# A GQA decode kernel's prologue reordered: q product between the two layer norms, constants ahead of x, residual copies behind the MLP's first half

## Chip, cores, metric

One core of one Trainium2 chip runs the whole program. The metric is the device time of one execution in microseconds (us); a median of several runs is given.

In the views PE is TensorE's matrix engine, PEld its weight loads, DVE VectorE, ACT ScalarE and SPq the queue of the SyncE. Evacuating is copying a result out of PE's output memory. The granted clock is the share of PE's full clock in the profile's records; half clock is a record of 0.5. L294 is the helper that waits for a semaphore.

## The reference

One decode step for four sequences: a layer norm `xn` of `x`; attention of `xn @ wq` with 16 query heads over 8 cached K/V heads of 8192 rows by 256; an MLP block on `xn`; the two are multiplied and added to `x`.

```python
xn = _layernorm(x)                       # x: (4, 1, 448)
s = _A_ref(xn, k_cache, v_cache, wq, wo) # K and V caches: (4, 8, 8192, 256) each, bf16
#   q = xn @ wq;  p = softmax(q k^T / 16);  o = p v;  s = o @ wo
g = _silu(_B_ref(xn, w1, w2, w3, w4))
#   x1 = xn + (shifted gelu(...)) ;  g = x1 + gelu(layernorm(x1) @ w3) @ w4
#   with one position the shifts leave only zeros, so x1 = xn and w1, w2 are not needed
return x + s * g
```

The K and V caches are 32 tiles each of 4.19 MB: 268 of the 279 MB that the program reads.

## The kernel before

A short prologue makes q and the MLP; then PE transposes each K tile, multiplies it with q and multiplies the probabilities with V. One queue (the SyncE's) issues all loads but that of x, in one fixed order:

```python
# SyncE: wq, w3, w4, then
load_k(0); load_k(1)                  # K0 (in two halves) and K1: no wait
load_wo(NLATE, HQ, "dwo")             # most of wo: no wait
for h in range(2, NH):
    load_k(h)                         # waits v_k >= h - 1: tile h-2 has been evacuated
    load_v(h - 2)                     # waits v_v: the V buffer is free
```

The prologue on VectorE (DVE), in the old order, and PE's part beside it:

```python
c(v.memset(q_ps[:, 0:QW], 0.0))
v.wait_ge(S["dx"], 16)
c(v.tensor_copy(x_f[:, :], x_sb[:, :]))
layernorm(x_f, xn_f, xn_b, 0, 1)          # each: sums, a square root on ACT, six copies
layernorm(xn_f, xn2_f, xn2_b, 8, 2)
c(v.tensor_reduce(par[:, :], idv, AX.X, ALU.add))
for k, dst in ((0, xnT), (1, xn2T)):      # four multiplications for each turn
    v.wait_ge(S["p_x"], k + 1)
    ...
# four memsets; sel, selb (reductions of the identity)
v.wait_ge(S["p_q"], 1)
v.tensor_copy(q_b[:, :], q_ps[:, 0:QW])   # then the residual copies x4, xn4
v.wait_ge(S["p_h"], 1)                    # MLP: gelu_u, tanh on ACT, hT, second product ...
...
# PE: turn xn, turn xn2, q product (28 matmuls), MLP's first product (49), q's transposes,
#     MLP's second product (14), a sum (4), four warm-up products (result unused), then K0's transposes
```

Of the kernel before, what the change touches and what calls it, by code (L numbers as in the profile page):

```python
# [7 lines left out]
ALU = mybir.AluOpType  # L8
AX = mybir.AxisListType
# [54 lines left out]
def bass_recurrent_scan__gqa_block_cached__mixer_s_mlp__decode_kernel(  # L64
# [13 lines left out]
    Bn, Sq, D = A_x.shape  # L78
    _, HKV, SK, DH = A_k_cache.shape
    HD = A_wq.shape[1]  # L80
    HQ = HD // DH
    REP = HQ // HKV
    F = B_w3.shape[1]
    assert Sq == 1 and REP == 2 and DH == 2 * P and HD == HQ * DH
    NHF = 2
# [6 lines left out]
    NQD = 4  # L92
    NDG = 2
    DQ, PQ = D // NDG, P // NQD
    DP = NDG * PQ
    assert D == NDG * DQ
    NCH = SK // P
# [12 lines left out]
    NCG = 4  # L110
    CGW = P // NCG
    CP = 2
# [23 lines left out]
    with ExitStack() as es:  # L136
        def sb(name, shape, dty):
# [7 lines left out]
        ident_f = sb("ident_f", [P, P], F32)  # L145
# [6 lines left out]
        selb = sb("selb", [P, PQ], F32)  # L152
        q_b = sb("q_b", [P, QW], BF16)
        pT = sb("pT", [P, 2, NCH * REP + PVW], BF16)
        xnT = sb("xnT", [P, DK, NHF, Bn], BF16)
        xn2T = sb("xn2T", [P, DK, NHF, Bn], BF16)
        par = sb("par", [P, NHF], F32)
        hT = sb("hT", [P, NFK, NHF, Bn], BF16)
        sel = sb("sel", [P, CP, PVW], F32)
# [11 lines left out]
        x_f = sb("x_f", [Bn, D], F32)  # L171
        xn_f = sb("xn_f", [Bn, D], F32)
        xn_b = sb("xn_b", [Bn, DK, P // 2, 2], BF16)
        xn2_f = sb("xn2_f", [Bn, D], F32)
        x4 = sb("x4", [DP, DQ], F32)
        xn4 = sb("xn4", [DP, DQ], F32)
        sg4 = sb("sg4", [DP, DQ], F32)
        res = sb("res", [DP, DQ], F32)
        xn2_b = sb("xn2_b", [Bn, DK, P // 2, 2], BF16)
# [6 lines left out]
        psc = [es.enter_context(nc.psum_tensor("psc%d" % i, [P, 512], F32)) for i in range(2)]  # L186
        psm = es.enter_context(nc.psum_tensor("psm", [P, 512], F32))
        psv = es.enter_context(nc.psum_tensor("psv", [P, 512], F32))
# [13 lines left out]
                                                                k=NFK)  # L202
# [15 lines left out]
                                                 r=REP)  # L218
# [74 lines left out]
        def take(eng, name, n=1):  # L293
            return eng.wait_ge(S[name], n).then_inc(S[name], -n)  # L294

        NPI, NPC = 4, 13

        def prog_pool(gp):
            c = _Chain(gp, S["g_c"])
            c(gp.memset(ident_f[:, :], 0.0))  # L300
            c(gp.memset(ident_b[:, :], 0.0))
            c.sync()
            for t in (ident_b, ident_f):
                c(gp.affine_select(out=t[:, :], in_=t[:, :], compare_op=ALU.not_equal, fill=1.0,
                                   base=0, pattern=[[-1, P]], channel_multiplier=1))
            c(gp.memset(ones_f[:, :], 1.0))
            c(gp.memset(diag[:, :], 0.0))
            c(gp.memset(sel[:, :, :].rearrange("p c n -> p (c n)"), 0.0))
            c(gp.memset(rz[:, :, :].rearrange("p s r -> p (s r)"), 1.0))
            gp.wait_ge(S["v_c"], 2)  # L310
            c(gp.memset(pT[:, :, :].rearrange("p s n -> p (s n)"), 0.0))
            for i in range(2):
                c(gp.memset(po[:, i], 0.0))
            c(gp.memset(qT_all[:, NH * TW:], 0.0))
            c(gp.memset(OT_all[:, :], 0.0))
            assert c.n == NPC
# [47 lines left out]
        def prog_dve(v):  # L364
            c = _Chain(v, S["v_c"])

            def layernorm(src_f, dst_f, dst_b, c0, k):
                col = lambda i: st[:, c0 + i:c0 + i + 1]
                c(v.tensor_reduce(col(0), src_f[:, :], AX.X, ALU.add))
                c(v.tensor_tensor_reduce(out=junk[:, :], in0=src_f[:, :], in1=src_f[:, :],  # L370
                                         scale=1.0, scalar=0.0, op0=ALU.mult, op1=ALU.add,
                                         accum_out=col(6)))
                v.wait_ge(S["v_c"], c.n - 1)
                c(v.tensor_scalar(col(4), col(0), 1.0 / D, None, op0=ALU.mult))
                c.sync()
                c(v.tensor_tensor(col(5), col(4), col(4), ALU.mult))
                c.sync()
                c(v.scalar_tensor_tensor(out=col(7), in0=col(6), scalar=1.0 / D, in1=col(5),
                                         op0=ALU.mult, op1=ALU.subtract))
                c.sync()  # L380
                v.tensor_scalar(col(1), col(7), LN_EPS, None, op0=ALU.add).then_inc(S["v_w"], 1)
                v.wait_ge(S["a_c"], k)
                c(v.reciprocal(col(3), col(2)))
                c.sync()
                c(v.tensor_scalar(dst_f[:, :], src_f[:, :], col(4), col(3),
                                  op0=ALU.subtract, op1=ALU.mult))
                c.sync()

                sv = dst_f[:, :].rearrange("b (m s) -> b s m", s=DK)
                nj = DK // 2  # L390
                for t in range(2):
                    pair = dst_b[:, t:2 * nj + t, :, t].rearrange("b (s u) m -> b s u m", u=2)
                    for u in range(2):
                        c(v.tensor_copy(pair[:, :, u, :], sv[:, t * (nj + 1):t * (nj + 1) + nj]))
                    c(v.tensor_copy(dst_b[:, (1 - t) * (DK - 1), :, t], sv[:, nj]))  # L395



            c(v.memset(q_ps[:, 0:QW], 0.0))
            v.wait_ge(S["dx"], 16)  # L400
            c(v.tensor_copy(x_f[:, :], x_sb[:, :]))
            c.sync()
            layernorm(x_f, xn_f, xn_b, 0, 1)
            xn_mark = c.n
            layernorm(xn_f, xn2_f, xn2_b, 8, 2)
            xn2_mark = c.n
            v.wait_ge(S["g_c"], NPI)
            idv = ident_f[:, :].rearrange("p (m t) -> p t m", t=NHF)
            c(v.tensor_reduce(par[:, :], idv, AX.X, ALU.add))
            c.sync()  # L410
            for k, dst in ((0, xnT), (1, xn2T)):
                v.wait_ge(S["p_x"], k + 1)

                for t in range(NHF):
                    for a in range(NHF):
                        ins = v.tensor_scalar(dst[:, t:DK:2, a, :], xT_ps[:, k, t:DK:2, :],
                                              par[:, (a + t) % 2:(a + t) % 2 + 1], None,
                                              op0=ALU.mult)
                ins.then_inc(S["v_xT"], 1)


            c(v.memset(psc[1][:, 0:NCH * REP], 0.0))
            c(v.memset(psv[:, 0:CP * DH], 0.0))
            for t in (x4, xn4):
                c(v.memset(t[:, :], 0.0))
            c.sync()
            v.sem_inc(S["v_po"], 1)
            v.sem_inc(S["dv0"], 16)
            v.sem_inc(S["dv1"], 16)
            v.wait_ge(S["g_c"], NPC)  # L430
            for i in range(CP):
                c(v.tensor_reduce(sel[:, i, 0:REP], ident_f[:, :].rearrange(
                    "p (j r) -> p r j", j=NCG)[:, i * REP:(i + 1) * REP], AX.X, ALU.add))
            c(v.tensor_reduce(selb[:, :], ident_f[:, :].rearrange("p (j r) -> p r j", j=NQD),
                              AX.X, ALU.add))
            v.wait_ge(S["p_q"], 1)
            v.tensor_copy(q_b[:, :], q_ps[:, 0:QW]).then_inc(S["v_qb"], 1)
            for src, dst in ((x_f, x4), (xn_f, xn4)):
                for i in range(NDG):
                    c(v.tensor_copy(dst[i * PQ:i * PQ + Bn, :], src[:, i * DQ:(i + 1) * DQ]))  # L440

            v.wait_ge(S["p_h"], 1)
            c(v.tensor_copy(gel_u[:, :], h_ps[:, 0:NF * Bn]))
            c.sync()
# [8 lines left out]
            for m in range(NQD):  # L453
# [10 lines left out]
            c.sync()  # L464
            v.tensor_tensor(hT[:].rearrange("p k a b -> p (k a b)"), gel_b[:, :], gel_u[:, :], ALU.mult
                            ).then_inc(S["v_hT"], 1)

            v.wait_ge(S["p_h2"], 1)
            v.tensor_copy(ou_f[:, :], h2_ps[:, 0:D]).then_inc(S["v_h2"], 1)
# [88 lines left out]
            c(v.tensor_tensor(res[:, :], o_ps[0:DP, 0:DQ], sg4[:, :], ALU.mult))  # L558
            c.sync()
            v.tensor_tensor(out_b[:, :], res[:, :], x4[:, :], ALU.add).then_inc(S["v_out"], 1)  # L560
            return xn_mark, xn2_mark

        def prog_pe(pe, xn_mark, xn2_mark):
            pe.wait_ge(S["g_c"], NPI)
            for k, (src, mark) in enumerate(((xn_b, xn_mark), (xn2_b, xn2_mark))):
                pe.wait_ge(S["v_c"], mark)
                for j in range(DK):
                    ins = pe.transpose(xT_ps[:, k, j, :],  # L568
                                       src[:, j].rearrange("b m t -> b (m t)"),
                                       ident_b[0:Bn, 0:Bn])  # L570
                ins.then_inc(S["p_x"], 1)
                if k == 0:
                    take(pe, "v_xT")
            take(pe, "dwq", 16)
            pe.wait_ge(S["g_c"], NPC)
            for j in range(DK):
                for i in range(NQD):
# [2 lines left out]
                                    wq_sb[:, j, i * QW:(i + 1) * QW],  # L580
                                    start=(j == 0), stop=(j == DK - 1))
            ins.then_inc(S["p_q"], 1)
            take(pe, "dw3", 16)
            take(pe, "v_xT")
            w3v = w3_sb.rearrange("p j (m k) -> p j k m", k=NFK)
            for k in range(NFK):
                for j in range(DK):
# [10 lines left out]
            for k in range(NFK):  # L598
                for a in range(NHF):
                    i = k * NHF + a  # L600
# [195 lines left out]
        marks, ahead = [], []  # L796
# [14 lines left out]
        @block.vector  # L811
        def _(v):
            marks.extend(prog_dve(v))
# [35 lines left out]
```

## Time and profile before

| | before |
|---|---|
| time, six runs | 653.74 us (653.21 to 654.18) |
| span of the profiled run | 651.9 us |
| PE, weight loads, DVE, ACT busy | 84%, 72%, 42%, 39% |
| first K transposes | 28.21 us |
| K2 (third K tile) issued | 41.65 us |

Busy shares are averages over the span; the prediction below shows the lines that carry it: the strip of DMA shares, four windows, the queue's issues and the prologue's rows. Two more views are needed later. First the end of the chain of work that ended last in the kernel before (start, length, what):

```profile
647.96 1.58 PE pst L721 x24
649.56 0.39 DVE res L558
```

The last 24 output products start before the last piece of wo has landed (648.98 in the DMA records) and end behind it: in this run the end hangs on the DMA. Second, the only gap of PE in the first K tile, as a row of the timeline; the bracket names the idle time before the group, and "issue" says that no wait is visible for it:

```profile
39.96 0.35 PE L634 MATMUL psc<-qc,kT 128*128 128x2 bf16 x8 [0.54 <-issue]
```

### The profile page before, as it was taken

To read this page: it belongs to the slowest core of one execution; us is meant where nothing else is said; L and a number is where in the kernel's file an instruction comes from. 1 tells how busy PE (TensorE), PEld (TensorE's weight loads), DVE (VectorE), ACT (ScalarE), POOL (GpSimd) and SP (SyncE) were. 2 spreads that over 40 slices of the span, in tenths; PEclk is the share of its full clock that TensorE was granted. 3 is DMA by queue.
4 is the path that set the end of the run, shared out by engine and by line. 5 is a ranking of instruction groups with operands and counts; after the bars stand their busy time and mean duration, and the time that the engine had idled before them with its cause. 6 is when DMAs were issued, how large, how long until landed. Compare 5 with 4: busy or idle time off the path is not lost. (4 is left out here: it accounts for less than half of the span.)

```text
span 651.9 us, 22794 instructions
## 1 busy us (share of the span) xinstructions
PE 550.5 (84%) x9927; PEld 472.3 (72%) x9927; DVE 276.8 (42%) x622; ACT 256.2 (39%) x364; POOL 3.6 (1%) x17
## 2 busy tenths in 40 slices
PE   1898997988888988878997887898788798878898
PEld 0586886977676887757877775797677688757785
DVE  6453554443344443434343443434344344434442
ACT  3253553443333443423443342444234344423340
POOL 2000000000000000000000000000000000000000
PEclk9998999888789877989897798979779987978999
DMA  9999999999999999999999999999999999999997
GB/s 379 440 418 438 423 442 426 440 428 434 434 432 436 426 440 420 446 422 444 424 441 426 438 430 434 434 432 436 424 440 422 444 424 442 426 442 426 438 428 299
DMA packets 12498, 279.13 MB, mean 428 GB/s; under 512 B 1221, under 2 KB 3273, under 8 KB 3785
## 3 DMA queue, kind: packets, MB, share of 16 engines
q1 hardware_dynamic: 12472, 278.99, 99.5%
q8 instruction: 7, 0.11, 0.1%
q14 instruction: 3, 0.02, 0.0%
q10 hardware_dynamic: 16, 0.01, 0.0%
HBM read 278.99 MB, written 0.00 MB: 428 GB/s over the span
## 5 line engine op out<-in xcount | busy, mean ns | idle before, releaser
L622 PE MATMUL pst<-ident_b,kn 128*128 128x128 bf16 x4096 | 344.7, 238 | 78.2 <-PEq L294 77.2
L325 ACT ACTIVATE kT<-pst 128x1024 bf16<-128x1024 bf16 x224 | 229.5, 1025 | 356.0 <-ACTq L294 354.8
L622 PEld LDWEIGHTS pst<-ident_b,kn 128*128 128x128 bf16 x4096 | 273.7, 107 | 84.3 <-issue 83.7
L323 DVE COPY kT<-pst 128x1024 bf16<-128x1024 bf16 x288 | 197.5, 691 | 257.4 <-DVEq L294 257.4
L634 PE MATMUL psc<-qc,kT 128*128 128x2 bf16 x4096 | 178.0, 164 | 0.5 <-issue 0.5
L634 PEld LDWEIGHTS psc<-qc,kT 128*128 128x128 bf16 x4096 | 156.8, 98 | 29.0 <-issue 28.8
L673 PE MATMUL psv<-vb,pT 128*4 128x512 bf16 x1056 | 87.2, 381 | 1.4 <-issue 1.4
L652 PE MATMUL psm<-sel,po 128*128 128x2 f32 x272 | 36.8, 257 | 0.5 <-PEq L294 0.5
L652 PEld LDWEIGHTS psm<-sel,po 128*128 128x128 f32 x272 | 34.8, 196 | 0.9 <-issue 0.9
L673 PEld LDWEIGHTS psv<-vb,pT 128*4 128x4 bf16 x1056 | 22.3, 82 | 16.6 <-issue 2.5
L482 DVE TENSOR_REDUCE rmax<-psc 128x2 f32<-128x128 f32 x32 | 9.3, 291 | 49.9 <-DVEq L294 49.9
L500 DVE COPY po<-psv 128x512 f32<-128x512 f32 x34 | 23.5, 692 | 3.0 <-DVEq L294 2.3
L487 DVE TENSOR_REDUCE gmax<-psm 2x1 f32<-2x128 f32 x32 | 8.9, 279 | 33.2 <-DVEq L294 33.2
L347 ACT ACTIVATE pT<-psc,negb 128x64 bf16<-128x64 f32 x66 | 20.6, 333 | 5.4 <-ACTq L294 5.4
L646 PEld LDWEIGHTS psm<-diag,ones_f 2*128 2x128 f32 x66 | 14.1, 265 | 6.5 <-issue 5.4
L646 PE MATMUL psm<-diag,ones_f 2*128 2x2 f32 x66 | 16.9, 323 | 1.0 <-PEq L294 0.9
L347 ACT ACTIVATION_READ_ACCUMULATOR pT<-psc,negb 128x1 f32 x66 | 13.6, 206 | 0.0
L642 PEld LDWEIGHTS psm<-ident_f,rmax 128*2 128x2 f32 x32 | 2.6, 80 | 14.4 <-issue 14.4
L568 PE MATMUL pst<-ident_b,xn_b 4*128 4x4 bf16 x14 | 0.6, 161 | 14.4 <-DVE xn_b L395 9.7
L664 PE MATMUL psm<-rowsum,ones_f 128*128 128x2 f32 x64 | 11.6, 251 | 0.0
L568 PEld LDWEIGHTS pst<-ident_b,xn_b 4*128 4x128 bf16 x14 | 0.5, 100 | 14.4 <-issue 9.7
L664 PEld LDWEIGHTS psm<-rowsum,ones_f 128*128 128x128 f32 x64 | 9.5, 188 | 0.0
(101 smaller groups left out, 104.9 us busy)
## 6 DMA issues: line engine op xcount, KB each, us to landing
kn<-in_A_k_cache_dram SPq DMA_DIRECT2D x31, 4096.0 KB, 24.8
vb<-in_A_v_cache_dram SPq DMA_DIRECT2D x31, 4096.0 KB, 30.4
kn<-in_A_k_cache_dram SPq DMA_DIRECT2D x2, 2048.0 KB, 24.5
vb<-in_A_wq_dram SPq DMA_DIRECT2D x1, 3584.0 KB, 11.3
vb<-in_B_w_dram SPq DMA_DIRECT2D x2, 1568.0 KB, 15.7
wo_sb<-in_A_wo_dram SPq DMA_DIRECT2D x1, 2688.0 KB, 42.5
kn<-in_A_v_cache_dram SPq DMA_DIRECT2D x1, 2048.0 KB, 24.8
kn<-in_A_v_cache_dram SPq DMA_DIRECT2D x1, 1024.0 KB, 26.8
```

The source lines that it names most:

```text
L323: engine.tensor_copy(dst, src).then_inc(S["v_ev"], 1)
L325: engine.activation(dst, src, ACT.Copy).then_inc(S["a_ev"], 1)
L347: ins = act.activation(pv_p[:, :, hh], sc[:, :, hh], ACT.Exp, bias=negb[:, s, hh:hh + 1], scale=SCALE, accum_out=rowsum[:, s, hh:hh + 1])
L482: v.tensor_reduce(rmax[:, :], psc[h % 2][:, 0:NCH * REP].rearrange("p (k h) -> p h k", h=REP), AX.X, ALU.max).then_inc(S["v_rmax"], 1)
L487: v.tensor_reduce(gmax[:, :], psm[0:REP, 0:P], AX.X, ALU.max).then_inc(S["v_s"], 1)
L500: v.tensor_copy(po[:, slot], psv[:, 0:CP * DH]).then_inc(S["v_po"], 1)
L622: ins = pe.transpose(dst[:, t * P:(t + 1) * P], kn[:, h % 2, GC * j + kl, half * P:(half + 1) * P], ident_b[:, :])
L634: ins = pe.matmul(psc[h % 2][:, kk * REP:(kk + 1) * REP], kT[:, j % RING, t * P:(t + 1) * P], qc[:, h % 2, half, :], start=(half == 0), st ...
L646: pe.matmul(psm[:, P:P + REP], ones_f[0:REP, :], diag[:, :], start=True, stop=True).then_inc(S["p_m2"], 1)
L652: ins = pe.matmul(dst(dh)[:, 0:width], po[:, slot, i * DH + dh:(i + 1) * DH:NHALF], sel[:, i, 0:width], start=(i == 0), stop=(i == CP - 1))
L664: pe.matmul(psm[:, P + REP:P + 2 * REP], ones_f[:, :], rowsum[:, h % 2, :], start=True, stop=True)
L673: ins = pe.matmul(psv[o:o + CP * REP, 0:CP * DH], pT[:, h % 2, kk * REP:(kk + CP) * REP], src[:, kk:kk + CP, :].rearrange("p c d -> p (c d)"),
```

## The change

Its intent is a shorter chain to the first K tile: q no longer stands between the MLP's inputs and its first product, VectorE makes its constants while x is under way, and the residual copies go where VectorE waits for PE.

```diff
+            c(v.memset(psc[1][:, 0:NCH * REP], 0.0))       # + psv, x4, xn4
+            v.wait_ge(S["g_c"], NPV)                       # identity and sel are written
+            c(v.tensor_reduce(par[:, :], idv, AX.X, ALU.add))
+            # ... sel (twice) and selb, moved here from behind the turns
             v.wait_ge(S["dx"], 16)
             c(v.tensor_copy(x_f[:, :], x_sb[:, :]))
-            layernorm(x_f, xn_f, xn_b, 0, 1)
-            layernorm(xn_f, xn2_f, xn2_b, 8, 2)
-            for k, dst in ((0, xnT), (1, xn2T)):
+            for k, (src, mid, turned, dst) in enumerate(((x_f, xn_f, xn_b, xnT),
+                                                         (xn_f, xn2_f, xn2_b, xn2T))):
+                layernorm(src, mid, turned, 8 * k, k + 1)
                 v.wait_ge(S["p_x"], k + 1)
                 # (four multiplications)
             v.tensor_copy(q_b[:, :], q_ps[:, 0:QW]).then_inc(S["v_qb"], 1)
-            for src, dst in ((x_f, x4), (xn_f, xn4)):      # moved behind hT
-                for i in range(NDG):
-                    c(v.tensor_copy(dst[i * PQ:i * PQ + Bn, :], src[:, i * DQ:(i + 1) * DQ]))
 # PE
-            (turn xn, turn xn2, q product, MLP's first product)
+            turn(0, xn_b, xn_mark)
+            (q product)
+            turn(1, xn2_b, xn2_mark)
+            (MLP's first product)
```

More of the change, by code (lines that the diff above doesn't have):

```diff
@@ L294, in take @@
             return eng.wait_ge(S[name], n).then_inc(S[name], -n)
-        NPI, NPC = 4, 13
+        NPI, NPV, NPC, NVX = 4, 7, 13, 10
         def prog_pool(gp):
@@ L309, in prog_pool @@
             c(gp.memset(rz[:, :, :].rearrange("p s r -> p (s r)"), 1.0))
-            gp.wait_ge(S["v_c"], 2)
+            gp.wait_ge(S["v_c"], NVX)
             c(gp.memset(pT[:, :, :].rearrange("p s n -> p (s n)"), 0.0))
@@ L399, in prog_dve @@
             c(v.memset(q_ps[:, 0:QW], 0.0))
+            c(v.memset(psc[1][:, 0:NCH * REP], 0.0))
+            c(v.memset(psv[:, 0:CP * DH], 0.0))
+            for t in (x4, xn4):
+                c(v.memset(t[:, :], 0.0))
+            v.wait_ge(S["g_c"], NPV)
+            idv = ident_f[:, :].rearrange("p (m t) -> p t m", t=NHF)
+            c(v.tensor_reduce(par[:, :], idv, AX.X, ALU.add))
+            for i in range(CP):
+                c(v.tensor_reduce(sel[:, i, 0:REP], ident_f[:, :].rearrange(
+                    "p (j r) -> p r j", j=NCG)[:, i * REP:(i + 1) * REP], AX.X, ALU.add))
+            c(v.tensor_reduce(selb[:, :], ident_f[:, :].rearrange("p (j r) -> p r j", j=NQD),
+                              AX.X, ALU.add))
             v.wait_ge(S["dx"], 16)
             c(v.tensor_copy(x_f[:, :], x_sb[:, :]))
+            x_mark = c.n
+            assert x_mark == NVX
             c.sync()
-            layernorm(x_f, xn_f, xn_b, 0, 1)
-            xn_mark = c.n
-            layernorm(xn_f, xn2_f, xn2_b, 8, 2)
-            xn2_mark = c.n
-            v.wait_ge(S["g_c"], NPI)
-            idv = ident_f[:, :].rearrange("p (m t) -> p t m", t=NHF)
-            c(v.tensor_reduce(par[:, :], idv, AX.X, ALU.add))
-            c.sync()
-            for k, dst in ((0, xnT), (1, xn2T)):
+            marks = []
+            for k, (src, mid, turned, dst) in enumerate(((x_f, xn_f, xn_b, xnT),
+                                                         (xn_f, xn2_f, xn2_b, xn2T))):
+                layernorm(src, mid, turned, 8 * k, k + 1)
+                marks.append(c.n)
                 v.wait_ge(S["p_x"], k + 1)
@@ L419, in prog_dve @@
                 ins.then_inc(S["v_xT"], 1)
-            c(v.memset(psc[1][:, 0:NCH * REP], 0.0))
-            c(v.memset(psv[:, 0:CP * DH], 0.0))
-            for t in (x4, xn4):
-                c(v.memset(t[:, :], 0.0))
             c.sync()
@@ L430, in prog_dve @@
             v.wait_ge(S["g_c"], NPC)
-            for i in range(CP):
-                c(v.tensor_reduce(sel[:, i, 0:REP], ident_f[:, :].rearrange(
-                    "p (j r) -> p r j", j=NCG)[:, i * REP:(i + 1) * REP], AX.X, ALU.add))
-            c(v.tensor_reduce(selb[:, :], ident_f[:, :].rearrange("p (j r) -> p r j", j=NQD),
-                              AX.X, ALU.add))
             v.wait_ge(S["p_q"], 1)
             v.tensor_copy(q_b[:, :], q_ps[:, 0:QW]).then_inc(S["v_qb"], 1)
-            for src, dst in ((x_f, x4), (xn_f, xn4)):
-                for i in range(NDG):
-                    c(v.tensor_copy(dst[i * PQ:i * PQ + Bn, :], src[:, i * DQ:(i + 1) * DQ]))
             v.wait_ge(S["p_h"], 1)
@@ L466, in prog_dve @@
                             ).then_inc(S["v_hT"], 1)
+            for src, dst in ((x_f, x4), (xn_f, xn4)):
+                for i in range(NDG):
+                    c(v.tensor_copy(dst[i * PQ:i * PQ + Bn, :], src[:, i * DQ:(i + 1) * DQ]))
             v.wait_ge(S["p_h2"], 1)
@@ L560, in prog_dve, with turn @@
             v.tensor_tensor(out_b[:, :], res[:, :], x4[:, :], ALU.add).then_inc(S["v_out"], 1)
-            return xn_mark, xn2_mark
+            return marks
         def prog_pe(pe, xn_mark, xn2_mark):
             pe.wait_ge(S["g_c"], NPI)
-            for k, (src, mark) in enumerate(((xn_b, xn_mark), (xn2_b, xn2_mark))):
+            def turn(k, src, mark):
                 pe.wait_ge(S["v_c"], mark)
@@ L571, in prog_pe @@
                 ins.then_inc(S["p_x"], 1)
-                if k == 0:
-                    take(pe, "v_xT")
+                take(pe, "v_xT")
+            turn(0, xn_b, xn_mark)
             take(pe, "dwq", 16)
@@ L582, in prog_pe @@
             ins.then_inc(S["p_q"], 1)
+            turn(1, xn2_b, xn2_mark)
             take(pe, "dw3", 16)
-            take(pe, "v_xT")
             w3v = w3_sb.rearrange("p j (m k) -> p j k m", k=NFK)
```

## The prediction

> **What bounds the kernel now.** I read the views from the outside in: first the page's strip of 40 slices, then busy times in chosen windows, then the DMA queue's own instructions in order of time, last the prologue's instructions in order of time.
>
> The strip (share of the 16 DMA engines that is busy, in tenths, and what they move):
>
> ```profile
> DMA  9999999999999999999999999999999999999997
> GB/s 379 440 418 438 423 442 426 440 428 434 434 432 436 426 440 420 446 422 444 424 441 426 438 430 434 434 432 436 424 440 422 444 424 442 426 442 426 438 428 299
> ```
>
> The DMA is full in the first slice (0 to 16.3 us), where the whole of the changed code begins, and in every other but the last. 279.13 MB at the page's mean of 428 GB/s are 652 us, which is the span of 651.9 us. The windows cut it by stage (columns: PE, weight loads, VectorE, ScalarE, GpSimd busy; then granted clock, DMA share, GB/s):
>
> ```profile
> 1.03:28.21 27.18, 11.10 (x117) 5.52 (x118) 16.69 (x68) 8.70 (x8) 3.44 (x13) 1.00 1.02 424
> 28.21:46.18 17.97, 17.38 (x320) 15.08 (x319) 7.73 (x18) 7.82 (x12) 0.00 (x0) 1.00 1.02 418
> 46.18:100.00 53.82, 50.73 (x998) 43.45 (x999) 26.70 (x57) 26.56 (x41) 0.00 (x0) 0.97 1.00 433
> 100.00:600.00 500.00, 425.35 (x7734) 370.84 (x7731) 206.65 (x438) 197.03 (x279) 0.00 (x0) 0.88 1.00 433
> ```
>
> The first row is the prologue: PE works 11 of 27 us there, VectorE 17, so it is a latency chain on the compute side; yet the DMA share is 1.0. In the long middle PE, the busiest compute engine, works 425 of 500 us. So the DMA queue sets the pace from the first packets (about 1 us) to the last landing (649 us), and the end is a tail of about 3 us of output product, two VectorE operations and the store. A change to the prologue can help only if the prologue makes that queue run dry. So the question is when the queue gets its next transfer:
>
> ```profile
> 3.19 0.47 SPq L251 DMA_DIRECT2D kn<-in_A_k_cache_dram  x1
> 3.70 0.49 SPq L276 DMA_DIRECT2D wo_sb<-in_A_wo_dram  x1
> 41.65 0.33 SPq L251 DMA_DIRECT2D kn<-in_A_k_cache_dram  x1
> 45.75 0.33 SPq L259 DMA_DIRECT2D vb<-in_A_v_cache_dram  x1
> 57.72 0.33 SPq L251 DMA_DIRECT2D kn<-in_A_k_cache_dram  x1
> ```
>
> By 4.2 us all of wq, w3, w4, the first two K tiles and most of wo are queued: no wait of the prologue stands in front of them. Then the queue waits for the evacuations of the first K tile (K0), and the third K tile (K2) is issued at 41.65. The DMA view gives wo 42.5 us from issue to landing, so wo ends at 3.70 + 42.5 = 46.2: the third K tile is issued 4.5 us before the queue would be empty. In the packet records the first wo share ends on one engine at about 44, and a K packet starts there at 43.95, 2.3 us after its issue, with no visible gap. This is the closest moment of the whole run: in the steady part K is issued far earlier (the last K tile at 592.62, while its own landing is at 617.5 and a tile takes 9.7 us, so some 15 us of other tiles lay before it).
>
> [...]
>
> **The change part by part.** The chain to the first K tile in the kernel before, from the timeline:
>
> ```profile
> 10.02 0.60 DVE L370 CUSTOM_DVE_ANT_0 junk<-xn_f 4x448 f32<-4x448 f32 x1
> 13.64 0.27 DVE L409 TENSOR_REDUCE par<-ident_f 128x2 f32<-128x128 f32 x1
> 13.95 0.62 DVE L416 TENSOR_SCALAR xnT<-pst,par 128x16 bf16<-128x16 bf16 x4
> 14.96 3.16 PE L578 MATMUL pst<-vb,xnT 128*8 128x512 bf16 x28
> 18.05 2.77 PE L588 MATMUL pst<-xn2T,vb 128*128 128x8 bf16 x49
> 26.36 1.91 PE L612 MATMUL psv<-vb,pT 128*32 128x512 bf16 x4
> 28.21 1.89 PE L622 MATMUL pst<-ident_b,kn 128*128 128x128 bf16 x16
> ```
>
> The q product (3.16 us) runs after both norms and delays the MLP's first product, which starts when it ends.
>
> 1. Constants forward. Four memsets (0.17 + 0.48 + 0.24 + 0.24), par 0.27, two sel 0.24, selb 0.37: 2.0 us, with the gaps about 2.2. VectorE is free from 1.77 (its first memset ends) to 4.92 (x lands), and GpSimd has written the identity and sel by 2.50. I put the constants at 1.8 to 4.0. So x's copy still starts at 4.92, set by the DMA of x; nothing added. Removed from the later path: par's 0.27 ahead of the transposed copies.
> 2. q between the norms. First norm's bf16 copies end at 9.57 as before. PE's seven transposes run 9.7 to 10.03 as before, the four multiplications (0.62) now at once, 10.06 to 10.70. VectorE stands idle about 0.5 us for the transposes. The second norm, 9.49 to 13.72 before (4.2 us), then runs 10.7 to 14.9. The q product starts at 11.4 rather than 14.96, as wq lands at 11.3 (DMA view), and ends at 14.5. The second turn: transposes 14.95 to 15.3, multiplications to 15.95. w3 landed at 15.05 (1.11 issue, its semaphore full then). So the first MLP product starts at about 16.0 instead of 18.05: **2.05 us sooner**. Sum: minus 3.1 (q product out of the chain), minus 0.3 (par), plus about 1.3 net (the second norm starts 1.2 later, and its own turn, 1.1 us of transposes and multiplications, now lies in front of the product, where before the first norm's turn, 1.0, did).
> 3. Residual copies back. 0.55 + 0.56 = 1.1 us; before they ran 18.78 to 19.93, inside PE's first MLP product, for which VectorE waited 0.94 us more. After they start at about 21.0, behind hT, inside the second product (1.66 us on PE, 21.1 to 22.8). They end at 22.2, before VectorE is needed at 22.8. Hidden both times: 0.
>
> So the first K transposes should start at 28.21 - 2.05, about **26.2 us**; the first K half landed at 24.0 and the second at 29.8, while its first use moves from 34.4 to 32.4, so neither holds it. K2's issue moves from 41.65 to about **39.6**. This is 2 us less of latency on PE, and 2 us more of reserve in the queue. On the DMA, which sets the end, the sum is 0: same bytes, same order, same descriptors, already full. The 2 us are spent as waiting: PE's third body starts at 63.6 though its K landed at 55.8, and it catches up at K4 (landed 94.6, PE idle 0.65 us for it); there PE will wait 2 us longer, and from about 95 us on the two kernels should coincide.
>
> **The rivals.**
> - *The queue does run dry near 44 us in the kernel before.* Then up to 2 us (0.3%) would come back: 651.5 us. For it: 41.65 is the closest approach, 2.3 us from issue to first packet. Against it: the share in 28.21 to 46.18 is 1.02, and by the packet records at least 14 of 16 engines are busy in every quarter microsecond from 2 to 646. The 418 GB/s there is wo's small packets (1792 bytes, 386 GB/s while they run), which stay. I give a gain over 1 us about 6%.
> - *A wait takes the place of the one removed.* ScalarE's fill of the spare vb ends (5.18 us) waits behind the second square root, which moves from 11.27 to 12.5; fill to 17.7, table load 1.28 to 19.05. The tanh is wanted at about 19.8 (before: 21.84). It fits by 0.7 us. If it missed, the prologue would gain only 1 to 1.5 us, and the total would still be 653.5.
> - [...] Granted clock is 1.0 up to 60 us, 0.88 in the middle; even a further fall leaves PE below the 38.7 us of a pair of heads. Effect on the total below 0.3 us.
> - *The gain passes through whole*, as it would if compute set the end: 651.5. The strip and the windows speak against it.
>
> **Range and chances.** The sum is 0, and with a tenth off for the first rival I put 653.4. The three runs before spread by 0.6 us; for another program image and the luck of which DMA engine finishes last (the last landing differs by 2.4 us between the engines, 646.5 to 649.0) I allow some 0.8 either way, a little more downward for the first rival: 652.6 to 654.2. Two per cent are 13 us, far more than the whole of what is moved: faster 0.01, same 0.985, slower 0.005.
>
> **What would show it right or wrong.** Right: q product at about 11.4, first MLP product at about 16.0, first K transposes at about 26.2, K2 issued at about 39.6, DMA strip unchanged, landings after 46 us unchanged within 0.3 us, a longer wait of PE at K4. Wrong in a step: the first MLP product after 17 (the turn or the norm costs more than I put), or the tanh waiting for its table. Wrong in the main: landings after 46 us sooner by 1 us or more (the queue was dry), or a dip in the DMA strip that was not there.

(Two passages are cut from this record, as they lean on what no trace or run of this case shows: a paragraph ahead of the change part by part, and the title of the rival about the granted clock. No term of the forecast's sum is cut: 2.05 us off the prologue, 0 on the DMA. What the argument needs of the paragraph is measured in the kernel before: 433 GB/s at a DMA share of 1.00 from 100 to 600 us, no load issued between 4.2 and 41.65 us at a share of 1.02, and two table loads on ACT, at 1.10 and 16.58, of 1.28 us each.)

## The result, and the profile after

The changed kernel took 653.68 us (median of six, 653.2 to 656.75), the kernel before 653.74. The ratio is 1.0007, 95% interval 0.9988 to 1.0027: the same. (A ratio is the mean time of one kernel's fast runs over that of the other's of the same rounds, so not quite the ratio of the medians.) The profiled run of the changed kernel spans 652.6 us.

Its prologue is shorter, as intended. The timeline's rows that answer to those in the prediction:

```profile
9.78 0.62 DVE L426 TENSOR_SCALAR xnT<-pst,par 128x16 bf16<-128x16 bf16 x4 [0.51 <-PE pst L569]
11.25 3.16 PE L580 MATMUL pst<-vb,xnT 128*8 128x512 bf16 x28 [1.51 <-PEq L294]
15.92 2.75 PE L590 MATMUL pst<-xn2T,vb 128*128 128x8 bf16 x49 [0.96 <-PEq L294]
24.21 1.91 PE L614 MATMUL psv<-vb,pT 128*32 128x512 bf16 x4
26.05 1.38 PE L624 MATMUL pst<-ident_b,kn 128*128 128x128 bf16 x16
```

The q product starts at 11.25 instead of 14.96, the MLP's first product at 15.92 instead of 18.05, K0's transposes at 26.05 instead of 28.21: 2.16 us won. The strip of the DMA and two of the windows:

```profile
DMA  9999999999999999999999999999999999999996
GB/s 380 443 414 436 427 436 428 440 428 440 428 440 428 438 430 436 432 434 434 434 431 430 434 432 436 430 438 428 440 428 440 428 436 430 438 428 440 428 428 285
...
28.21:46.18 17.97, 15.86 (x287) 12.33 (x285) 6.65 (x15) 7.00 (x11) 0.00 (x0) 0.84 1.01 416
...
100.00:600.00 500.00, 425.34 (x7736) 370.82 (x7733) 206.78 (x438) 196.92 (x279) 0.00 (x0) 0.89 1.00 433
```

The DMA was full before and is full now, at the same 433 GB/s. By the landing records K2, K3 and K4 arrive at 55.90, 75.24 and 94.63 us, before at 55.84, 75.17 and 94.58. So the won time went to where the prediction put it, a longer stay in the queue. But the queue's rows show something that it did not foresee:

```profile
3.75 0.49 SPq L276 DMA_DIRECT2D wo_sb<-in_A_wo_dram  x1
40.18 0.33 SPq L251 DMA_DIRECT2D kn<-in_A_k_cache_dram  x1
46.13 0.33 SPq L259 DMA_DIRECT2D vb<-in_A_v_cache_dram  x1
61.28 0.33 SPq L251 DMA_DIRECT2D kn<-in_A_k_cache_dram  x1
```

K2's issue came only 1.47 us sooner (40.18 for 41.65), and V0 and K3 were issued later than before (46.13 for 45.75, 61.28 for 57.72). PE had lost its lead within the first tile. Two losses of time stand in the trace. One is a longer gap in K0's work, where the kernel before had 0.54 us:

```profile
38.49 0.35 PE L636 MATMUL psc<-qc,kT 128*128 128x2 bf16 x8 [2.12 <-issue]
```

The other is the granted clock, from two windows of 2 us taken at the same place, first the kernel before, then the changed one (the third number from the right):

```profile
42.00:44.00 2.00, 2.00 (x46) 1.05 (x47) 0.50 (x3) 0.00 (x0) 0.00 (x0) 1.00 1.08 420
```
```profile
42.00:44.00 2.00, 2.00 (x26) 0.67 (x24) 0.37 (x2) 0.00 (x0) 0.00 (x0) 0.50 1.06 406
```

PE was busy for all of both windows but did 26 matmuls instead of 46. The clock records give the changed kernel half clock from 40.4 to 47.2 and from 54.1 to 60.9; the kernel before had none from 30.9, where its records begin, until 61.7. And the end of the changed kernel's chain begins earlier and lies on PE:

```profile
647.38 1.10 PE pst L775 x8
648.47 0.39 PE pst L733 x16
648.87 1.46 PE pst L723 x24
```

The same 24 products start 0.9 us later than before, though the last landing was 0.2 us sooner (648.82). That is the 0.8 us by which the profiled span is longer (652.63 for 651.85).

### The profile page after: what moved, and what is told of

The parts are those of the page before. It is cut to its first block, busy times and chain, and to the rows that moved or that the text cites. A ratio compares the mean times of both kernels' runs of the same rounds, so it can differ in the third digit from the quotient of the medians.

```text
span 652.6 us, 22794 instructions
## 1 busy us (share of the span) xinstructions
PE 553.5 (85%) x9927; PEld 474.8 (73%) x9927; DVE 276.6 (42%) x622; ACT 256.2 (39%) x364; POOL 3.6 (1%) x17
## 5 line engine op out<-in xcount | busy, mean ns | idle before, releaser
L491 DVE TENSOR_SCALAR diag<-ident_f,gmax 2x2 f32<-2x2 f32 x32 | 6.9, 217 | 4.8 <-DVEq L294 1.4
```

## The experiments

Theory A: the DMA queue is full from about 2 to 646 us, so the prologue's 2 us can't shorten the run; they only add to the reserve with which K2 is issued. Rivals: (B) the new order itself brings a longer gap and an early half clock, which eat a gain that would otherwise count; (C) compute latency passes through to the end. Eleven kernels ran; all were within the tolerance of the reference (the half tile too, although half of its K rows are another tile's). The wait of about 2.1 us in e1's expectation is that gap, 2.12 us in the first profile of the changed kernel.

**e1_after_again**: the changed kernel, unedited.

> The changed kernel once more, unedited, timed in five rounds beside the kernel before. Theory A (the DMA queue is full from 2 to 646 us, so the 2 us taken from the prologue are worth nothing; what differs between runs is the half-clock stretch that falls into the last K tile's work): ratio to before 1.000 +- 0.002, every landing from the third K tile (K2) on within 0.3 us of the kernel before, and the tail after the last landing 2.9 to 3.7 us according to whether the last tile's work had 3.4 or 6.8 us at half clock. Rival B (the gain was eaten by something that the new order brings by itself, such as [...] an early half-clock stretch at 40 us): the same wait of about 2.1 us and the same early half-clock stretch appear again, and K2 is again issued at 40.2 instead of 39.6; the total is 653.7 under both, the landings after 46 us decide.

Measured: 653.62 us, ratio 0.9999 (0.9985 to 1.0012). K2 landed at 55.90, K3 at 75.23, K4 at 94.57. The gap in K0's work was there again, with 1.02 us; K2 was issued at 40.34. The early half clock was not: the first came at 53.3 us, for 3.4 us. So the longer gap came back, but shorter, and the early half clock did not. The half clock at 53.3 cost PE its lead for a while (K3 was issued at 57.89, before at 57.72); the kernel before then had its own at 61.7, and by K4 the changed kernel was 3.0 us ahead (issue at 72.80 for 75.80). PE's wait for K4 shows it; three rows, of the kernel before, the changed kernel and this run:

```profile
94.71 1.05 PE L622 MATMUL pst<-ident_b,kn 128*128 128x128 bf16 x16 [0.65 <-PEq L294]
```
```profile
94.77 1.05 PE L624 MATMUL pst<-ident_b,kn 128*128 128x128 bf16 x16 [0.31 <-PEq L294]
```
```profile
94.70 1.54 PE L624 MATMUL pst<-ident_b,kn 128*128 128x128 bf16 x13 [3.64 <-PEq L294]
```

All three start K4 at 94.7, when it has landed; what PE won or lost before is taken up by the wait.

**e4_half_k16**: the kernel before with 2.1 MB less to load (the result is wrong, if by little).

```diff
-                sp.dma_start(kn_dst(h), A_k_cache[b, g].rearrange("(p c) d -> p (c d)", p=P)
+                n = NCH * DH // (2 if h == 16 else 1)
+                sp.dma_start(kn_dst(h)[:, 0:n],
+                             A_k_cache[b, g].rearrange("(p c) d -> p (c d)", p=P)[:, 0:n]
```

> The kernel before, but of the 17th K tile (K16) only half is loaded (2.1 MB less; the result is wrong on purpose). Theory A (bytes on the DMA queue set the end): 2.097 MB / 433 GB/s = 4.8 us shorter, 648.7, and all landings after K16's 4.8 us sooner. Rival (compute or its waits set the pace in the middle): no change, as all instructions on the compute engines are the same.

Measured: 648.41 us beside 653.38, 4.97 us less (ratio 0.9924, 0.9909 to 0.9939), with every compute instruction still there. Bytes in the queue set the end; a compute-paced middle is ruled out.

**e2_delay_before** and **e3_delay_after**: 16 memsets on VectorE ahead of the copy of the MLP's second product, in the kernel before and in the changed one. The edit is the same in both:

```diff
             v.wait_ge(S["p_h2"], 1)
+            for _ in range(16):
+                c(v.memset(junk2[:, :], 0.0))      # 128 x 512 float32
+                c.sync()
```

> The kernel before with 16 extra memsets (about 0.51 us each, so 8.2 us) on VectorE ahead of the copy of the second MLP product, which holds up the first K tile's work by as much. K2's issue should move from 41.65 to about 49.9. wo's last packets end at 44.0 to 46.2 on the 16 engines, 45 in the mean, and the first packet of an idle queue came 1.0 us after its issue at the start. Theory A: the DMA share shows a hole of about 6 us near 45 to 51, every later landing and the total are 6 us later (the reserve of the kernel before is some 2.3 us of the 8.2). Rival (compute latency passes through whole): 8.2 us. Rival (the prologue is free at any length): 0.

> The changed kernel with the same 8.2 us of memsets at the same place. K2's issue from 40.2 to about 48.4. Theory A: a hole of about 4.5 us, so total 4.5 us longer, and 1.5 us (the 41.65 - 40.18 that the change won for K2's issue[...]) shorter than the delayed kernel before: the change's gain is real and becomes visible once the queue runs dry. Rival (the change wins no time that could ever count): the same time as the delayed kernel before.

Measured: 661.45 us (ratio 1.012, 1.0104 to 1.0135) and 660.59 us (1.0102, 1.0086 to 1.0117) beside 653.38. A memset with its wait took 0.66 us, not 0.51, so the delay was 10.5 us, not the 8.2 of the expectation. K2's issue in the first, and its windows from 44 us on:

```profile
50.54 0.33 SPq L252 DMA_DIRECT2D kn<-in_A_k_cache_dram  x1
```
```profile
44.00:46.00 2.00, 2.00 (x36) 2.00 (x33) 0.87 (x2) 1.07 (x2) 0.00 (x0) 1.00 0.23 84
46.00:48.00 2.00, 2.00 (x53) 2.00 (x50) 0.76 (x2) 1.16 (x2) 0.00 (x0) 1.00 0.00 0
48.00:50.00 2.00, 2.00 (x53) 2.00 (x51) 1.03 (x4) 1.73 (x2) 0.00 (x0) 1.00 0.04 8
50.00:52.00 2.00, 2.00 (x44) 1.22 (x41) 1.17 (x2) 0.18 (x1) 0.00 (x0) 1.00 0.84 229
```

This is what a dry queue looks like: share 0.00 while PE is busy all the time. Counted over the 16 engines, loads alone, the hole is 7.29 us in the first and 6.53 in the second (0.10 in the undelayed kernel before). K2's issue came 8.89 us later than before in the first and at 49.71 in the second; K3 landed at 83.67 and 82.68, 8.5 and 7.5 us late, and the totals went with it, 8.1 and 7.2 us. The landings lag 1.0 to 1.2 us more than the hole: the first packet came 1.0 us after the issue, and the first 16 packets (15 in the second), all 32 KB, took 1.4 to 2.4 us each instead of 1.21. So with the queue dry, the change is worth 0.83 us at K2's issue, 1.0 at the landings and 0.9 in the medians: by sign what A says, but only half of the 1.76 us between the two kernels' first K transposes (38.43 and 36.67), and less than the 1.5 expected. The rest, 0.93 us, went in K0's first 32 transposes: they took 2.97 us in the first and 3.90 in the second, whose record of full clock begins 3.4 us after K0's start (at 40.1), against 1.3 (at 39.7). So how much of the 1.76 arrives went here with the moment at which that record begins, and there is one profile of each. (The intervals of the totals overlap; it is the landings that show it.) And of the 8.9 us at K2's issue 8.1 reached the total of the kernel before: it had little reserve.

**e7_short_delay_before** and **e8_short_delay_after**: 4 memsets instead of 16.

> The kernel before with 4 of the extra memsets (0.66 us each by the long delay's trace, so 2.6 us). K2's issue from 41.65 to about 44.2, its first packet (1.0 us after issue on an empty queue, as the long delay showed) at 45.2, while the engines run out of wo between 43.9 and 45.3. Theory A': the reserve of the kernel before is 1.3 us on the first engine and some 2 in the mean, so 2.6 us make a hole: 0.5 to 0.9 us of idle DMA time between 43 and 54 us, and with the slow restart that the long delay showed (landings 1.1 us later than the hole) K3's landing 1 to 2 us later than the 75.2 of the undelayed kernel. Rival (reserve of 3 us or more): landing at 75.2.

> The changed kernel with the same 4 memsets. K2's issue from 40.2-40.3 to about 42.8, first packet possible at 43.8, before any engine is out of wo. Theory A': no hole, K3 lands at 75.2 as without a delay, total as the kernel before: the change's whole worth is that the queue now tolerates some 1.4 us more. Rival ([...] an early half-clock stretch eats the reserve): a hole as in the delayed kernel before.

Measured: 656.65 us (654.64 to 658.84; ratio 1.0045, 1.0027 to 1.0063) and 654.30 us (1.0009, 0.9996 to 1.0022) beside 653.49. The queue's K2 issue and the two thin windows of the delayed kernel before:

```profile
44.52 0.33 SPq L252 DMA_DIRECT2D kn<-in_A_k_cache_dram  x1
```
```profile
44.00:45.00 1.00, 1.00 (x26) 0.75 (x23) 1.00 (x2) 0.00 (x0) 0.00 (x0) 0.92 0.50 192
...
65.00:66.00 1.00, 1.00 (x22) 0.51 (x19) 0.69 (x1) 0.00 (x0) 0.00 (x0) 0.84 0.19 66
```

The first hole is 1.16 us at K2, as A expected. The second was not expected: K3 was issued at 65.18, when V0 was already running out, and another 0.69 us were lost; K3 landed at 79.48, 4.3 us late. The issues of the delayed changed kernel:

```profile
41.95 0.33 SPq L252 DMA_DIRECT2D kn<-in_A_k_cache_dram  x1
...
61.40 0.33 SPq L252 DMA_DIRECT2D kn<-in_A_k_cache_dram  x1
```

No hole at K2 (0.11 us), but K3 landed at 75.71, 0.5 us late: issued 2.3 us before the first engine had finished V0, many of the packets up to 68 us were slow (16 of 32 KB over 1.3 us, one in the undelayed kernel before) with no idle time. So the same 2.6 us cost the kernel before 3.2 us, and the changed one 0.8 us by the medians, with an interval that holds none; the two intervals do not meet. Here the change shows its worth, but not by the reserve alone. The first hole is the reserve's. But K3's late issue in e7 also has half clock in front of it, from 44.8 to 51.7 and from 58.5 to 65.3, where e8 has it from 54.0 to 60.8 alone. How much of the 2.4 us between the medians is reserve and how much clock, these runs do not separate.

**e5_q_only, e6_without_q, e9_copies_undone**: one part alone, or one undone (one run each; the kernel before took 653.67 beside them). e5 is the kernel before with the new loop and PE order and par ahead of the first norm; e6 the changed kernel with the old loop and PE order; e9 is the changed kernel with this (the loop itself cut, its place told):

```diff
+            # behind the copy of q: the residual copies x4, xn4
-            # behind hT: the residual copies x4, xn4
```

> The kernel before with the new order of the q product alone (par made ahead of the first norm, the other constants and the copies at their old places). By the prediction's sum the MLP's first product starts about 1.7 us sooner (16.35 instead of 18.05: par, 0.3 us, is back on VectorE's chain), but memsets, sel, selb, the q copy and the residual copies (3.7 us with gaps) now stand between the second turn and the MLP's first evacuation, which is free at about 20.0 instead of 19.2: first K transposes about 27.4, 0.8 us sooner than before, not 2.1. Rival (the parts simply add, q product 1.8 us): 26.4. Total within 0.3% of before.

> The changed kernel with the q product put back behind both norms: constants early and copies late, nothing else. Prediction's sum: par's 0.27 us only, so the MLP's first product at 17.8 and the first K transposes at 27.9 (27.6 if x lands as early as in the profile of the changed kernel, where its copy started 0.29 us sooner). Rival (constants and copies carry the gain): about 26.5. Total within 0.3% of before.

> The changed kernel with the residual copies back in their old place, behind the q copy. The prediction has them hidden in both places: VectorE waited 2.49 us for the MLP's first product there, the copies take 1.1: first K transposes at 26.1, as in the changed kernel. Rival (the copies delay the evacuation): 0.5 to 1.1 us later. Total within 0.3% of before.

Measured: first K transposes at 26.89, 27.96 and 25.99; totals 654.50, 653.18, 653.87. The copy gelu_u, the MLP's first evacuation, tells why; the rows of e5, e6, e9 in turn:

```profile
19.53 0.22 DVE L443 COPY gel_u<-pst 128x56 f32<-128x56 f32 x1
```
```profile
20.61 0.22 DVE L440 COPY gel_u<-pst 128x56 f32<-128x56 f32 x1 [1.93 <-PE pst L589]
```
```profile
18.65 0.22 DVE L444 COPY gel_u<-pst 128x56 f32<-128x56 f32 x1 [1.43 <-PE pst L590]
```

With q alone VectorE comes to it without a wait: it is late itself, held up by the constants and copies. The MLP's first product started at 16.02, 2.0 us sooner than before, but only 1.3 us reach K0 (0.5 of them by x, whose copy started at 4.41 in this run instead of 4.92). The constants moved forward free the other part; alone they bring 0.25. The copies' place is free either way, as long as the constants are gone: VectorE still waits 1.43 us with them in front.

**e10_no_warm** and **e11_after_third**: the changed kernel with `NWARM = 0` instead of 4, and unedited.

> The changed kernel without its four warm-up products (1.9 us on PE just ahead of the first K transposes), so that the first K tile starts at about 24.2 instead of 26.1, right behind its landing at 24.0. Theory A: nothing to win, ratio to before 1.000 +- 0.002, K2, K3 and K4 land at 55.9, 75.2, 94.6; K2's issue sooner by 1 to 1.9 us. Rival (a still shorter prologue does bring time): 1 us or more.

> The changed kernel, unedited, for the spread: one of its first six timed runs took 656.75 and one 654.56, while 26 runs of the kernel before stayed within 653.06 to 654.37. Theory A: both kernels have the same spread and 656.75 was a rare run (a K3 issued too late, as seen in the short delay of the changed kernel, would do it): five runs within 653.1 to 654.4. Rival (the changed kernel [...] spreads more): at least one of five over 654.4.

Measured: 654.08 us (ratio 1.0003, 0.9989 to 1.0017) and 653.78 us (1.0000, 0.9986 to 1.0013). Without warm-up K0's work began at 24.38 and K2 was issued at 39.08; K2, K3, K4 landed at 55.77, 75.11, 94.50. A still shorter prologue is worth nothing either. The five runs of e11 lie within 653.30 to 654.18, while the kernel before had one of 655.36 among nine: the larger spread of the changed kernel, suspected from 656.75, did not show again.

## Why the prediction was right

**The bound.** The prediction put 653.4 us (652.6 to 654.2), and 653.68 was measured. The mechanism is right too, and now shown both ways: taking 4.8 us of bytes out took 5.0 us off the time, and taking up to 4 us out of the prologue took nothing (e1, e10, e11).

**The prologue's sum.** Right to 0.15 us: the q product at 11.25 (11.4), the MLP's first product at 15.92 (16.0), first K transposes at 26.05 (26.2). One term was off: x's copy was set at 4.92 "by the DMA of x"; it started at 4.63, and between 4.41 and 4.99 in the runs, since x's landing itself varies by half a microsecond. So up to 0.3 us of the agreement is luck; with x's copy at 4.88 (e11) K0's work began at 26.30. The tanh did not wait for its table, which was loaded at 18.68 for a use at 19.69. The residual copies were hidden, as said.

**K2's issue.** Off by 0.6: 40.18 and 40.34 for the predicted 39.6 (39.34 in e11). The step "2 us less of latency on PE, and 2 us more of reserve" failed: the gap in K0's work grew from 0.54 to 2.12 and 1.02 us. In all eleven profiles that have this gap (0.54 to 2.49 us) it comes after the same 204 matmuls of K0, and in the DMA records a 16 KB packet of the queue that the page lists as "instruction" (q8, 7 packets, 0.11 MB) starts 2.2 to 2.4 us before PE goes on: at 37.62 in the kernel before, at 36.29 and 36.24 in the first two profiles of the changed one. PE reached the gap at 39.42 before and at 36.37 and 37.64 after, 3.0 and 1.8 us sooner, while the packet came only 1.3 and 1.4 sooner; the difference is the longer gap. What PE waits for in the gap is not shown: the view names no releaser, the packet is a coincidence in time, and no run took it away.

That PE won 3.0 us in one profile and 1.8 in another lies, by the estimate below, in the clock, which the prediction misread. It took the granted clock as "1.0 up to 60 us"; but the first record begins at 30.9 in the kernel before, and the view prints 1.00 also where it has no record. K0's first 16 transposes took 1.89 us there, as they did in e6 inside a recorded half clock (21.3 to 31.5), and 1.05 later at full clock (the row at 94.71 above). The record of full clock begins 2.7 us after K0's start in the kernel before, 0.7 and 3.2 us after it in the two profiles of the changed one. If the clock was 0.50 until then, that is 1.0 us less and 0.3 more on the way to the gap (an estimate from these three times); measured from K0's start, the way took 11.2 us before, 10.3 and 11.4 after.

The early half clock goes with the gap's length: in the four profiles where it was 1.67 us or more (the changed kernel's first, e5, e7, e9) half clock of 6.8 us set in at 40 to 45 us, in the seven with 1.38 or less it did not between the gap and 51. So rival B was half right: time is lost on PE in the new order (the gap was 2.12, 1.02 and 0.84 in the changed kernel's three profiles, 0.54 in the kernel before and in e4), and gaps of 1.67 to 2.49 us were followed by 6.8 us of half clock. But it is not the new order's alone: e7, with the old order and a delay, had 1.94. Nor does the length of one gap decide alone: later, one of 0.79 us just before 52.5 was followed by 3.4 us of half clock (e1), and one of 1.01 us just before 53.7 was not (the kernel before). What does is not shown. The lost time ate the won time on PE; it ate none of the total, for there was none to eat.

**PE's wait at K4.** "There PE will wait 2 us longer" was wrong as a number: 0.65 us became 0.31, and 3.64 and 2.90 in later runs of the same kernel. An early half clock of 6.8 us takes more from PE (3.4 us, an estimate from 6.8 us at a recorded 0.50) than the change gives it. The conclusion, that the kernels coincide from 95 us on, held in all of them.

**The closest moment.** The reserve at K2 is not the 4.5 us that the prediction read from wo's landing: in e2, with K2 issued 8.89 us later, the queue stood empty for 7.29, so 1.6 were spare; in e5, with K2 issued at 42.27, it landed at 55.94 (55.84 before). And K2 is not the only such moment. K3's issue depends on how fast the first two tiles go; it ranged from 57.7 to 61.3 us in the profiles of the two kernels, and in e8 and e5, at 61.4 and 61.65, its slow start cost 0.5 and 0.8 us. Whether the run of 656.75 was such a case is open, as it has no profile.

**The clock at the end.** "Below 0.3 us" was too small. The time from the last landing to the end was 2.8 to 2.9 us in the eight profiles that had no half clock or 3.4 us of it in the last K tile's work, and 3.4 to 3.9 in the five with 6.8 us. In the changed kernel's first profile this is the 0.8 us of longer span. (The 2.4 us between the engines, which the range allows for, are 1.9 by the landing records of the last piece, 647.09 to 648.98.) The stretch of 6.8 us in the last K tile's work was seen only in the changed kernel and its variants (five of eight profiles, e6, e10 and e11 without it), in none of the five of the kernel before and its variants; whether that is chance these runs don't settle, and the ratios of the timed runs (1.0007, 0.9999, 1.0000) show no cost of it.

## What to carry to other kernels

As long as the queue of loads did not run dry, a shorter prologue bought reserve here and not time (first K transposes 2.16 us sooner, ratio 1.0007), so ask first at which moment the queue next waits for compute, and how long before its end that issue comes. A reserve has a value that a median does not show: the same disturbance of 2.6 us cost one kernel 3.2 us and the other 0.8, if in part by the clock. And moving one long step off a chain may only uncover the small ones behind it: the reordered product paid in full only after the constants had left VectorE's way (first K transposes at 26.89 in e5, with the product moved, and at 25.99 in e9, with the constants moved too; 28.21 before).
